# The splits of a first expert's weight pieces moved later, and a mask copy moved ahead of a copy of results, in a fused retention, mixture and attention kernel

## The chip, the core and the metric

The kernel runs on one core of a Trainium2 chip. The core has five engines that run side by side, each with its own in-order stream of instructions: TensorE (PE in the profile, with its weight loads as PEld), VectorE (DVE), ScalarE (ACT), GpSimd (POOL) and SyncE (SP, which here only issues DMA transfers). They meet through semaphores. The metric is the device time of one execution, in microseconds (us).

## The reference

Three layers follow one another, all in float32: a retention layer (a running state per head), a layer of eight experts in which each token goes to one expert, and an attention layer with four gated heads.

```python
def _attn_ref(q, k, v):                       # B, H, S, D = 2, 8, 768, 64
    for t in range(S):
        state = gamma * state + outer(k[:, :, t], v[:, :, t])
        y[:, :, t] = scale * (q[:, :, t] @ state)

def _moe_ref(x, w_gate, w_local, w1, w2):     # 8 experts, 512 -> 1024 -> 512
            fresh_e = int(np.argmax(logits[b, s]))
            e = fresh_e if s == 0 or local_gate[b, s] < 0.5 else prev_e
            prev_e = e
            h = np.maximum(x[b, s] @ w1[e], 0.0)
            out[b, s] = p[e] * (h @ w2[e])

def _moe2_ref(x, w_gate, wq, wk, wv, wo):     # 4 attention heads, each token weighs the top 2
```

The expert of a token can hang on the token before it (it keeps the last expert unless its local gate says otherwise), so the routing is a scan along the sequence.

## The kernel before

**Retention and routing.** The sequence is cut into six chunks of 128 positions, two batches each. A loop runs over the first five chunks; the sixth is written out by hand behind it. In chunk c the engines compute the outputs of chunk c (`outputs_past`, `outputs_now`), copy them out of PSUM (`evacuate`, on ACT), update the state (`state`, `keep`), and work on the routing of chunk c - 1 in a class `Route`: `first` (DVE) finds the mask of tokens that keep their expert and the fresh choices; `keeps` and `fresh` (PE) turn both masks; `spread` (ACT) copies the turned mask out of PSUM into `rs`; `held` and `count` (DVE) are scans along the tokens; `offset` (PE) adds the counts of earlier chunks; `rank`, `slots`, `hots` and `table` build the table of which token sits at which place of which expert. The table, the offsets and the places stand in one PSUM tile, pB, of which `pTab` is a part.

In the last chunk V is the routing of the fifth chunk, W that of the fourth and U that of the sixth. Once V's and W's part of the table is there, the rows of the first expert are gathered (`gather(0, GE)`, POOL), while U is still worked out; U's tokens are added to the gathered block by matmuls (`late`). The block is copied out as a high half x0h (ACT) and the remainder x0l (DVE).

**Weights in two halves.** Each expert's weights come in eight pieces of 128x1024 (pieces 0 to 3 of the first matrix, 4 to 7 of the second). `fetch_piece(i)` (SP) loads the raw piece into one of five buffers, `split_high(i)` (ACT) rounds it to `whi`, and `split_low(i)` (DVE) writes the remainder `wlo`. Three products stand for one: whi with the high half of x, wlo with it, and whi with the low half. Since raw buffers turn over five by five, piece 5 is loaded into the buffer that piece 0 leaves, 6 into that of 1, 7 into that of 2, 8 into that of 3, and a fetch waits until its forerunner's `split_low` has read it.

**Order.** The loop, the last chunk and the experts are recorded under a manual schedule: each engine runs its instructions in the order in which the code issues them. PSUM tiles of kind "B" rotate through three buffers: pS, pR and pB hold them in the first layer, then `warm`, then the four results `ph` of the first expert's first matrix, so that the second `ph` (piece 1) takes the buffer of pB and the fourth that of the first.

The first expert multiplies at L900 (first matrix, 24 matmuls a piece) and L948 (second matrix). Behind U's part of the table stand, on DVE, the ordering of the experts (`PM` to `OD`), a `split_low(2)`, the copy `tf` of the finished table out of pB (L781), the gather lists and `split_low(3)`.

Of the kernel before, what the change touches and what calls it, by code (L numbers as in the profile page):

```python
# [24 lines left out]
NC = S // C  # L25
# [87 lines left out]
def kernel(  # L113
# [57 lines left out]
    def fetch_piece(i):  # L171
        if i >= NP:
            return
        e, r = divmod(i, 8)
        raws[i] = ring.tile([128, 1040], F32, name="wraw", bufs=RAWS)[:, :1024]
        src = w1 if r < 4 else w2
        if e:
            if e > len(ords):
                n = slice(1, 2) if e == 1 else slice(2, E)
                ords.extend(nc.values_load_multi_w_load_instructions(  # L180
                    OD[0:1, n], engines=[mybir.EngineType.SP], min_val=0, max_val=E - 1)[1])
            src = src[bass.ds(ords[e - 1], 1), r % 4].rearrange("e p n -> (e p) n")
        else:
            src = src[e, r % 4]
        nc.sync.dma_start(raws[i], src)

    def split_high(i):
        hi = ring.tile([128, 1024], F32R, name="whi", bufs=PIECES)
        lo = ring.tile([128, 1024], F32R, name="wlo", bufs=PIECES)
        nc.scalar.activation(hi, raws[i], AF.Copy)  # L190
        pieces[i] = (hi, lo)

    def split_low(i):
        hi, lo = pieces[i]
        nc.vector.tensor_tensor(out=lo, in0=raws.pop(i), in1=hi.bitcast(F32), op=OP.subtract)  # L195
# [48 lines left out]
    with tc.tile_pool(name="s1", bufs=2) as s1:  # L244
# [9 lines left out]
        def load_pair(c, x):  # L254
            if c >= NC:
                return
            for b in range(B):
                load_half(c * B + b, x)
# [55 lines left out]
        def fade(n, j):  # L314
            nc.vector.tensor_tensor(out=AM[n][:, j], in0=PA[n][j], in1=DT[:, j], op=OP.mult)
# [26 lines left out]
        def outputs_past(c):  # L342
            pY = [bank("C", [128, 2 * B, C]) for _ in range(2)]
            if c:
                for b in range(B):
                    for g in range(2):
                        for r, j in ((0, 0), (1, 1), (0, 1), (1, 0)):
                            k = 2 * g + j
                            nc.tensor.matmul(pY[r][half(j), 2 * b + g, :], SB[b][half(r), k, :],
                                             QD[B * c + b][half(r), k * C:(k + 1) * C], start=b == 0 and g == 0, stop=False,  # L350
                                             skip_group_check=True)
            return pY

        def outputs_now(c, pY, r):
            for b in range(B):
                x = XB[B * c + b, 1]
                for g in range(2):
                    for j in range(2):
                        h = 4 * g + 2 * r + j
                        nc.tensor.matmul(pY[r][half(j), 2 * b + g, :], x[:, 1, h * D:(h + 1) * D],  # L360
                                         AM[B * c + b][:, r, 2 * g + j, :], start=c == 0, stop=True, skip_group_check=True)

        def evacuate(c, pY, r):
            XT[c, r] = s1.tile([128, 2 * B, C], F32, name="xT")
            nc.scalar.activation(XT[c, r], pY[r], AF.Copy)
# [4 lines left out]
        def state(n):  # L370
            c, b = divmod(n, B)
            if c == NC - 1:
                return
            for k in range(H // 2):
                for r in range(2):
                    h = k // 2 * 4 + r * 2 + k % 2
                    nc.tensor.matmul(pS[half(r), b, k, :], KD[n][:, h, :], XB[n, 1][:, 1, h * D:(h + 1) * D],
                                     start=c == 0 and b == 0 and k == 0, stop=True, skip_group_check=True)

        def keep(n):  # L380
            c, b = divmod(n, B)
            if c == NC - 1:
                return
            nc.scalar.activation(SB[b], pS[:, b], AF.Copy)
# [24 lines left out]
        def put_rows(pv):  # L409
            for dst, src in zip(rows_of(XRT[:, :, E:]), pv):  # L410
                nc.scalar.activation(dst, src, AF.Copy)

        def send_rows(n):
            c, b = divmod(n, B)
            t = b * S + c * C + 1
            nc.sync.dma_start(x1_d[t:t + C, :], XRT[:, b])
# [124 lines left out]
        with tc.manual_schedule(engines={ENG.PE, ENG.DVE, ENG.Activation, ENG.Pool, ENG.SP}):  # L541
# [11 lines left out]
            def turn(c):  # L553
                part, logits, pv = turn_pair(c)
                l2 = s1.tile([128, B, E + 1], F32, name="l2")
                part(0, 8)
                return lambda: [logits(b, l2) for b in range(B)], pv

            for c in range(NC - 1):
                load_pair(c + 2, 0)  # L560
                if c >= NC - 3:
                    fetch_piece(3 * (c - NC + 3))
                if c == NC - 2:
                    split_high(0)
                if c:
                    sums, pv = turn(c - 1)
                if c >= 2:
                    RT[c - 2].columns()
                    RT[c - 2].slots(0, B)
                    RT[c - 2].marks(0, B)  # L570
                    RT[c - 2].tokens(0, B)
                if c >= 3:
                    RT[c - 3].table(0, B)
                if c:
                    sums()
                    put_rows(pv)
                    for b in range(B):
                        send_rows(B * (c - 1) + b)
                    RT[c - 1] = Route(c - 1)
                    RT[c - 1].first(LL[c - 1], 0, B)  # L580
                if c >= 2:
                    RT[c - 2].hots(0, B)
                if c == NC - 2:
                    split_low(0)
                if c == 2:
                    nc.sync.dma_start(x1_d[0:1, :], ZR[0:1])
                    for b in range(B):
                        t = b * S + (NC - 1) * C + 1
                        nc.sync.dma_start(x1_d[t:t + C, :], ZR)
                ns = [B * c + b for b in range(B)]  # L590
                nn = [n + B for n in ns]
                pY = outputs_past(c)
                for r in range(2):
                    outputs_now(c, pY, r)
                    evacuate(c, pY, r)
                for n in ns:
                    state(n)
                if c:
                    RT[c - 1].keeps()
                    RT[c - 1].fresh()  # L600
                    RT[c - 1].spread()
                    RT[c - 1].held()
                    RT[c - 1].count()
                for n in ns:
                    keep(n)
                if c == NC - 2:
                    split_high(1)
                    split_high(2)
                for f in (decay_q, decay_k):
                    for n in nn:  # L610
                        f(n)
                load_pair(c + 2, 1)
                if c == 1:
                    nc.gpsimd.memset(ZR, 0.0)
                if c >= NC - 3:
                    for i in ((1, 2), (4,))[c - NC + 3]:
                        fetch_piece(i)
                next_qt(c + 2)
                scores(nn[0], "A")
                for r in range(2):  # L620
                    fade(nn[0], r)
                scores(nn[1], "C")
                if c:
                    RT[c - 1].offset()
                    RT[c - 1].rank()
                for r in range(2):
                    fade(nn[1], r)
                if c:
                    RT[c - 1].shares(LL[c - 1], 0, B)
            c = NC - 1  # L630
# [14 lines left out]
                fetch_piece(i)  # L645
            V = RT[c - 1] = Route(c - 1)
            V.first(LL[c - 1], 0, B)
            split_low(1)
            pY = outputs_past(c)
            U = Route(c)  # L650
            xs = [s1.tile([128, B, DM], F32R, name="blq", bufs=4) for _ in range(2)]
# [36 lines left out]
                                     start=False, stop=m == 1 and b == 1, skip_group_check=True)  # L688

            outputs_now(c, pY, 0)  # L690
            evacuate(c, pY, 0)
            V.keeps()
            V.fresh()
            V.spread()
            V.held()
            V.count()
            W.hots(0, B)
# [67 lines left out]
            for x in range(2):  # L765
                n = slice(2 * x, 2 * x + 2)
                nc.vector.tensor_tensor(out=X0[1][:, n, :], in0=acc[x], in1=X0[0][:, n, :].bitcast(F32),
                                        op=OP.subtract)
            nc.vector.tensor_tensor(out=PM, in0=rk[:, None, :].to_broadcast(sq),
                                    in1=cn("place")[:, :, None].to_broadcast(sq), op=OP.is_equal)  # L770
            one = s1.tile([1, 2, E, E], F32, name="one")
# [752 lines left out]
```

## Time and profile before

| | us |
|---|---|
| three runs | 388.18, 388.53, 390.83 (median 388.53) |
| the profiled execution, whole | 387.61 |
| its span in the trace | 385.8 |
| PE busy | 371.9 (96% of the span) |
| DVE busy | 282.8 (73%) |
| ACT busy | 233.4 (60%) |
| POOL busy | 123.3 (32%) |

All times of a trace are counted from the start of the span; an execution is 1.81 us longer than its span here (387.61 - 385.8). A busy share is a mean over layers with different limits. The retention layer ends at about 67 us of the span, the experts at about 250 us, and attention takes the rest. Rows of a timeline merge neighbours of one kind; the duration of a merged row reaches from the first start to the last end.

### The profile page before, as it was taken

What the parts mean: (1) busy time and instruction counts of PE and PEld (TensorE: products, weight loads), DVE (VectorE), ACT (ScalarE), POOL (GpSimd) and SP (SyncE); (2) the same over time, 40 slices, a digit from 0 to 9 for tenths busy, and PEclk for the clock granted to TensorE, in tenths of its full rate; (3) what the DMA queues carried; (4) which work ended last, traced back from release to release, by engine and by line L of the source; (5) the groups of instructions that cost most, each with busy time, mean ns of one, the idle gap of its engine ahead of it and who ended that gap; (6) DMA issues with size and microseconds to landing.
All of it is one profiled execution on the core that took longest, in us unless ns stands there. A gap on an engine that the chain in (4) does not pass through costs nothing.

```text
span 385.8 us, 8560 instructions
## 1 busy us (share of the span) xinstructions
PE 371.9 (96%) x3020; PEld 326.0 (84%) x3020; DVE 282.8 (73%) x783; ACT 233.4 (60%) x547; POOL 123.3 (32%) x172
## 2 busy tenths in 40 slices
PE   7999888999999999999999999999999999999993
PEld 3999777989989797889898898989889988988782
DVE  5589887885767868788888991578976876678741
ACT  1555563464647656587777781557866765759641
POOL 2775312151514022131310022434445422515420
PEclk9999999999999999999999999999999999999998
DMA  7999964696785667778776752131120001000111
GB/s 251 400 405 338 398 235 148 172 299 238 229 304 179 226 239 242 243 235 274 244 245 232 246 220 96 51 110 58 29 72 21 21 0 57 0 30 27 56 58 62
DMA packets 23610, 67.39 MB, mean 175 GB/s; under 512 B 4469, under 2 KB 4725, under 8 KB 23560
## 3 DMA queue, kind: packets, MB, share of 16 engines
q1 hardware_dynamic: 21010, 59.34, 44.9%
q0 software_dynamic: 2544, 7.42, 5.6%
q8 instruction: 26, 0.43, 0.4%
q14 instruction: 24, 0.20, 0.2%
q10 hardware_dynamic: 6, 0.01, 0.0%
HBM read 56.16 MB, written 11.07 MB: 174 GB/s over the span
## 4 chain that ended last, share of the span: by engine, by line
PE 88%; DMA 6%; issue 2%; DVE 1%; ACT 1%; SPq 0%; POOL 0%; POOLq 0%; ACTq 0%; DVEq 0%
PE C L948 19%; PE B L900 9%; PE C L1100 8%; PE B L912 5%; PE C L1285 5%; PE B L1265 5%; PE A L1209 4%; PE C L1138 4%; PE C L1306 4%; PE A L912 3%; PE C L360 3%; PE B L914 2%; PE C L944 2%; DMA x_d<-y,SI 2%; DMA blk<-in_blk_dram 2%
## 5 line engine op out<-in xcount | busy, mean ns | idle before, releaser
L195 DVE TENSOR_TENSOR wlo<-wraw,whi 128x1024 fp32r<-128x1024 f32 x64 | 77.0, 1223 | 15.7 <-ACT whi L190 15.6
L190 ACT ACTIVATE whi<-wraw 128x1024 fp32r<-128x1024 f32 x64 | 65.6, 1050 | 3.0 <-DMA wraw<-in_w_dram 2.9
L970 POOL DMA_INDIRECT x_d<-y,SI x16 | 19.9, 1243 | 125.1 <-ACT y L960 80.5
L1243 POOL TENSOR_SCALAR a<-a,mx,wt 128x128 f32<-128x128 f32 (+5 forms) x48 | 33.9, 716 | 51.5 <-PE B L1265 12.0
L1232 ACT ACTIVATE a<-a,mx 128x128 f32<-128x128 f32 (+5 forms) x48 | 32.2, 670 | 23.0 <-DVE mx L1222 19.6
L948 PE MATMUL C<-whi,hh 128*128 128x512 f32 (+4 forms) x112 | 45.5, 407 | 0.0
L948 PE MATMUL C<-whi,hl 128*128 128x512 f32 (+4 forms) x112 | 44.2, 394 | 0.0
L948 PE MATMUL C<-wlo,hh 128*128 128x512 f32 (+4 forms) x112 | 44.2, 394 | 0.0
L912 PE MATMUL B<-xx,whi 128*128 128x384 f32 (+3 forms) x100 | 31.0, 365 | 0.0
L1265 PE MATMUL B<-K,a 128*128 128x128 f32 x168 | 26.4, 274 | 0.0
L1222 DVE CUSTOM_DVE_ANT_0 a<-A,MR 128x384 f32<-128x384 f32 (+3 forms) x48 | 25.3, 530 | 1.5 <-PE A L1209 0.9
L914 PE MATMUL B<-xx,wlo 128*128 128x192 f32 (+3 forms) x100 | 25.5, 255 | 0.0
L948 PEld LDWEIGHTS C<-whi,hl 128*128 128x128 f32 (+4 forms) x112 | 20.0, 179 | 6.0
L948 PEld LDWEIGHTS C<-wlo,hh 128*128 128x128 f32 (+4 forms) x112 | 20.1, 180 | 5.0
L948 PEld LDWEIGHTS C<-whi,hh 128*128 128x128 f32 (+4 forms) x112 | 20.1, 179 | 4.7
L886 ACT ACTIVATE hh<-t 128x128 fp32r<-128x128 f32 (+4 forms) x56 | 16.3, 318 | 12.1 <-DVE t L918 11.8
L1265 PEld LDWEIGHTS B<-K,a 128*128 128x128 f32 x168 | 19.9, 140 | 2.6 <-issue 0.7
L224 POOL DMA_INDIRECT xg<-x_d,GI x14 | 16.4, 1173 | 17.5 <-DVE hl L902 13.5
L1209 PE MATMUL A<-ks,qh 128*128 128x256 f32 (+3 forms) x56 | 21.5, 384 | 0.0
L1285 PE MATMUL C<-at,vv 128*64 128x256 f32 (+1 forms) x204 | 20.6, 347 | 0.0
L912 PEld LDWEIGHTS B<-xx,whi 128*128 128x128 f32 x100 | 18.8, 188 | 0.7
L914 PEld LDWEIGHTS B<-xx,wlo 128*128 128x128 f32 x100 | 19.1, 191 | 0.2
(327 smaller groups left out, 963.1 us busy)
## 6 DMA issues: line engine op xcount, KB each, us to landing
wraw<-in_w_dram SPq DMA_DIRECT2D x64, 512.0 KB, 4.8
blq<-in_blk_dram SPq DMA_DIRECT2D x12, 512.0 KB, 8.6
blk<-in_blk_dram SPq DMA_DIRECT2D x12, 512.0 KB, 8.2
x_d<-xr SPq DMA_DIRECT2D x12, 260.0 KB, 6.0
out_dram<-y SPq DMA_DIRECT2D x12, 256.0 KB, 2.0
xr<-x_d SPq DMA_DIRECT2D x10, 256.0 KB, 2.6
x_d<-ZR SPq DMA_DIRECT2D x2, 260.0 KB, 5.4
wraw<-in_wv_dram SPq DMA_DIRECT2D x1, 520.0 KB, 5.8
```

The costliest lines, as they stand in the source:

```text
L190: nc.scalar.activation(hi, raws[i], AF.Copy)
L195: nc.vector.tensor_tensor(out=lo, in0=raws.pop(i), in1=hi.bitcast(F32), op=OP.subtract)
L900: nc.tensor.matmul(ph[:, a, :N], w[:, k, n], x[:, k, :N], start=m == 0, stop=m == 11)
L912: nc.tensor.matmul(pa[:, :, :N], wh[:, k, n], XX[e][:, k, :, :N], start=k == 0, stop=False, skip_group_check=True)
L914: nc.tensor.matmul(pa[:, 1, :N], wl[:, k, n], XX[e][:, k, 0, :N], start=False, stop=k == 3, skip_group_check=True)
L948: nc.tensor.matmul(pys[i][:rows], h[:, a, n], w[:, a, :], start=f == 0 and a == 0 and m == 0, stop=f == 3 and a == 1 and m == 2)
L1100: nc.tensor.matmul(pp, w[:, k, a * 128:(a + 1) * 128], x[:, k, :], start=m == 0, stop=m == 11)
L1209: nc.tensor.matmul(ps[:, :w], qq[b, g, e][:, tq], KS[b, e][:, s0:s0 + w], start=m == 0, stop=m == 1)
L1232: nc.scalar.activation(AA[u][:, :n], AA[u][:, :n], AF.Exp, bias=mx[:, 0, i:i + 1], scale=-1.0, accum_out=mx[:, 1, i:i + 1])
L1243: nc.gpsimd.tensor_scalar(a[:, :n], a[:, :n], mx[:, 1, i:i + 1], WT[b, g][:, i, e:e + 1], op0=OP.mult, op1=OP.mult)
L1265: nc.tensor.transpose(pT[:, s - s0, :], a[:, s * C:(s + 1) * C], ident)
L1285: nc.tensor.matmul(po[j * HD:(j + 1) * HD, r], VV[b, s][:, e * HD:(e + 1) * HD], at[j][:, s, r], start=s == 0, stop=s == ns - 1, skip_grou ...
```

## The change

The three high halves of pieces 0 to 2 are now all made behind the state copies of the fifth chunk (c == 4, `NC - 2`); before, the first stood at the start of that chunk. `split_low(0)` moves from the fifth chunk to the place in the last chunk where `split_low(1)` stood, and `split_low(1)` moves behind the two x0l subtractions, ahead of `PM`. In the last chunk, `V.spread()` now stands ahead of `evacuate(c, pY, 0)` on ACT.

```diff
@@ fifth chunk (c == NC - 2) @@
-                if c == NC - 2:
-                    split_high(0)
                 if c:
                     sums, pv = turn(c - 1)
...
                     RT[c - 2].hots(0, B)
-                if c == NC - 2:
-                    split_low(0)
...
                 for n in ns:
                     keep(n)
                 if c == NC - 2:
-                    split_high(1)
-                    split_high(2)
+                    for i in range(3):
+                        split_high(i)
@@ last chunk @@
             V.first(LL[c - 1], 0, B)
-            split_low(1)
+            split_low(0)
...
             outputs_now(c, pY, 0)
-            evacuate(c, pY, 0)
             V.keeps()
             V.fresh()
             V.spread()
+            evacuate(c, pY, 0)
             V.held()
...
                 nc.vector.tensor_tensor(out=X0[1][:, n, :], in0=acc[x], in1=X0[0][:, n, :].bitcast(F32),
                                         op=OP.subtract)
+            split_low(1)
             nc.vector.tensor_tensor(out=PM, in0=rk[:, None, :].to_broadcast(sq),
```

ACT, from the state copies of the fifth chunk (SB) to the exponentials of the last (PP); whi is a high half, xr the copy of the rows, rs the copy of the turned mask, xT the copies of results:

```order
 L384 ACTIVATE SB_119<-B 128x256
-L190 ACTIVATE whi<-wraw 128x1024 x2
+L190 ACTIVATE whi<-wraw 128x1024 x3
 L453 ACTIVATE PP,DN<-L,nm 128x8 x2
 L411 ACTIVATE xr<-C 128x384
 L411 ACTIVATE xr<-A 128x2x128
 L411 ACTIVATE xr<-A 128x384
-L365 ACTIVATE xT<-C 128x512
 L480 ACTIVATE rs<-B 128x128
-L365 ACTIVATE xT<-C 128x512
+L365 ACTIVATE xT<-C 128x512 x2
 L453 ACTIVATE PP,DN<-L,nm 128x8 x2
```

The third high half has come behind the state copies, and rs has passed the first of the two copies of results.

DVE, at the end of the last chunk, before the change; x0l is the low half of the gathered block, wlo a weight's low half (piece 2's here), tf the copy of the table out of pB:

```order
118 L767 TENSOR_TENSOR x0l<-C,x0h 128x512 x2
119 L769 TENSOR_TENSOR PM<-rk,K 128x64
120 L772 TENSOR_TENSOR one<-PM,K 1x64
121 L775 TENSOR_REDUCE pick<-one 1x8
122 L776 CAST OD<-pick 1x8
123 L195 TENSOR_TENSOR wlo<-wraw,whi 128x1024
124 L781 COPY tf<-B 128x16
```

The same place with the change:

```order
117 L763 TENSOR_TENSOR x0l<-C,x0h 128x512 x2
118 L195 TENSOR_TENSOR wlo<-wraw,whi 128x1024
119 L766 TENSOR_TENSOR PM<-rk,K 128x64
120 L769 TENSOR_TENSOR one<-PM,K 1x64
121 L772 TENSOR_REDUCE pick<-one 1x8
122 L773 CAST OD<-pick 1x8
123 L195 TENSOR_TENSOR wlo<-wraw,whi 128x1024
124 L778 COPY tf<-B 128x16
```

Piece 1's low half now stands between x0l and PM, so tf has two low halves ahead of it instead of one.

## Rows read from the trace of the kernel before

**Rows 1.** The page, part 4: the chain that ended last, by engine

```profile
PE 88%; DMA 6%; issue 2%; DVE 1%; ACT 1%; SPq 0%; POOL 0%; POOLq 0%; ACTq 0%; DVEq 0%
```

**Rows 2.** That chain from 53 to 92 us: start us, us, what

```profile
60.21 3.40 DMA xg<-x_d,GE
...
68.06 11.56 PE B L900 x94
...
85.21 0.44 PE A L835 x4
```

**Rows 3.** PE timeline, last chunk: start us, us, work [idle before, releaser]

```profile
54.86 0.22 PE L476 MATMUL B<-IB,fo 128*128 128x128 bf16 x1
...
57.14 0.16 PE L495 MATMUL B<-rc,OM 128*128 128x1 bf16 x1 [1.04 <-DVE oh L525]
```

**Rows 4.** ACT timeline, last chunk

```profile
54.97 0.60 ACT L365 ACTIVATE xT<-C 128x512 f32<-128x512 f32 x1 [0.76 <-PE C L360]
55.46 0.27 ACT L480 ACTIVATE rs<-B 128x128 f32<-128x128 f32 x1
```

**Rows 5.** DVE timeline, last chunk

```profile
54.23 1.22 DVE L195 TENSOR_TENSOR wlo<-wraw,whi 128x1024 fp32r<-128x1024 f32 x1
55.77 0.48 DVE L485 TENSOR_TENSOR_SCAN rc<-rs,rc,B 128x128 bf16<-128x128 f32 x1 [0.32 <-ACT rs L480]
```

**Rows 6.** Timelines of DVE and PE, fifth chunk

```profile
47.68 1.21 DVE L195 TENSOR_TENSOR wlo<-wraw,whi 128x1024 fp32r<-128x1024 f32 x1
...
49.32 0.42 DVE L489 TENSOR_TENSOR_SCAN rc<-B,rc 128x128 bf16<-128x128 f32 x1
...
50.29 0.18 PE L495 MATMUL B<-rc,OM 128*128 128x2 bf16 x1
```

**Rows 7.** ACT timeline, fifth chunk and start of the last

```profile
44.22 0.49 ACT L411 ACTIVATE xr<-C 128x384 f32<-128x384 f32 x1 [0.25 <-DVE l L398]
...
48.78 2.02 ACT L190 ACTIVATE whi<-wraw 128x1024 fp32r<-128x1024 f32 x2
...
52.49 0.30 ACT L453 ACTIVATE PP<-L,nm 128x8 f32<-128x8 f32 x1 [1.70 <-DVE nm L451]
```

**Rows 8.** DVE timeline, end of the last chunk and first expert

```profile
68.65 0.22 DVE L769 TENSOR_TENSOR PM<-rk,K 128x64 f32<-128x64 f32 x1
...
69.46 1.21 DVE L195 TENSOR_TENSOR wlo<-wraw,whi 128x1024 fp32r<-128x1024 f32 x1
70.60 0.15 DVE L781 COPY tf<-B 128x16 f32<-128x16 f32 x1
...
74.95 0.69 DVE L902 SCALAR_TENSOR_TENSOR hl<-B,hh 128x512 fp32r<-128x512 f32 x1 [0.88 <-DMA x_d<-PP]
```

**Rows 9.** PEld timeline, the first expert's first matrix

```profile
70.18 0.54 PEld L900 LDWEIGHTS B<-x0l,whi 128*128 128x128 f32 x4
70.81 0.53 PEld L900 LDWEIGHTS B<-x0h,whi 128*128 128x128 f32 x4
71.27 0.55 PEld L900 LDWEIGHTS B<-x0h,wlo 128*128 128x128 f32 x4
...
76.49 0.55 PEld L900 LDWEIGHTS B<-x0h,whi 128*128 128x128 f32 x4
```

**Rows 10.** SP queue timeline; landing of line L416 there; the page, part 6

```profile
65.79 0.82 SPq L416 DMA_DIRECT2D x_d<-xr  x2
70.70 0.34 SPq L185 DMA_DIRECT2D wraw<-in_w_dram  x1
...
DMA to landing us min/median/max: 2.1/2.3/2.7
...
x_d<-xr SPq DMA_DIRECT2D x12, 260.0 KB, 6.0
```

**Rows 11.** POOL timeline: the gather for the second expert

```profile
76.05 1.96 POOL L224 DMA_INDIRECT xg<-x_d,GI  x1 [13.53 <-DVE hl L902]
```

**Rows 12.** Stretch 56 to 57.2: us, PE, PEld, DVE, ACT, POOL busy, PEclk, DMA, GB/s

```profile
56.00:57.20 1.20, 0.16 (x5) 0.15 (x3) 1.13 (x5) 0.60 (x2) 0.00 (x0) 1.00 0.79 258
```

## The prediction

> **What bounds the kernel now.** I read the chain that ended last first: PE carries 88% of it [rows 1], so what the change is worth is what it does to PE's start in the stage that it touches, and whether PE waits behind that. The piece of the chain for that stage shows two things. From the last chunk's routing to the first expert the chain runs through small steps, and a gather of 3.40 us stands in it [rows 2]; a step ahead of the gather that ends earlier brings all of it forward. From 68.06 us on PE runs through L900, L948 and the turning of the next expert's rows at 85.21 [rows 2], so a delay of PE behind 68 us is not made up for there, and one ahead of it is carried on as well. The timelines of the single engines then tell what each step waits for.
>
> Two waits of PE matter. At 57.14 the offset matmul starts after 1.04 us without work, and its releaser is the last DVE step of a row that starts from the copied mask rs [rows 3]: rs, the two scans, the mask table `oh`. And at 70.81 the first weight load of piece 1 is late: groups of four loads follow each other at 0.46 (70.81 to 71.27), so it was due at about 70.64, behind 70.18; it came 0.06 after the table copy tf ended (70.60 + 0.15 = 70.75) [rows 8, 9]. The result `ph` of piece 1 takes the PSUM buffer of pB, which tf reads last. So PE already waits, for some 0.15 us, on the place in DVE's stream into which the change puts another low half.
>
> **The fifth chunk: nothing.** The first high half leaves ACT's stream ahead of xr, but xr waited for DVE's logits anyway, with 0.25 us of idle time in front of it [rows 7]; nothing is gained. Made as a third copy behind the state copies, at the spacing of the two there ((2.02 - 1.05) = about 0.97 us each), it ends near 51.8, and ACT next has work at 52.49, after 1.70 us without any [rows 7]. The cover is that wait for DVE; without it the price would be 0.97 us on ACT. On DVE a low half of 1.21 us goes, which stood between the mask table and the scans [rows 6]. The second scan ended at 49.74 (49.32 + 0.42), and PE asked for it at 50.29, in its own order, with no wait [rows 6]. So an earlier scan brings PE nothing: 0, where the bound would be one low half, 1.14 us, had PE been waiting there.
>
> **rs ahead of the copy of results: a gain of 0.34 us.** rs started at 55.46, 0.49 behind xT, though the masks on PE ended at 55.08 (54.86 + 0.22) [rows 3, 4]. Put first, it can start at about 55.12 (a releaser's step costs 0.04 here) and end at 55.39, not 55.73. The scan `held` behind it started at 55.77 after 0.32 us of waiting for rs [rows 4, 5]. It can now start at 55.43; DVE's low half (now piece 0's, of the same size) lets the next step in by 54.23 + 1.14 = 55.37 [rows 5], so the low half nearly binds but does not. Gain: 55.77 - 55.43 = 0.34 us. The bounds are 0 (if the low half ends later than that) and 0.40. The gain reaches PE, since the offset waits for this row, and PE has been without other work since 56.10 (57.14 - 1.04) [rows 3]; then all up to the gather and its 3.40 us follows PE. The copy of results that rs passes ends by 55.99 (55.39 + 0.60), and its first reader, the gate's matmuls, stands behind the offset at 56.80, so it hides there.
>
> **Piece 1's low half ahead of PM: a loss of 1.14 us.** It stands in front of four small steps, then piece 2's low half, then tf. One low half holds DVE for 1.14 us from its start to the next step's (69.46 to 70.60) [rows 8]. All of it is DVE time with no idle stretch to take it up, and tf moves by it in full, against the x0l ahead of it. Counted with the gain, x0l ends 0.34 earlier, the low half runs from 68.31 (68.65 - 0.34) to 69.45, and tf ends at 70.75 - 0.34 + 1.14 = 71.55. PE has finished piece 0 at 70.64 - 0.34 = 70.30, and waits for 1.3 us instead of 0.15; its load starts at 71.61, not 70.81.
>
> The spacing comes from the row. The Trainium skill (VectorE: DVE Perf Modes, section "The DRAIN you can't avoid") says that the next operation doesn't start until the pipe has emptied, which would make the price the full duration, 1.21 us, and the net loss 0.87; the trace shows the next step starting 0.07 us ahead of that end, so its 1.14 stands.
>
> Does PE make that up later? Its next gates move by the same amount. The fourth result's load at 76.49 needs the first `hl`, which ended at 75.64 (74.95 + 0.69), 0.85 us earlier [rows 8, 9]; both move by 0.80. The low halves of the second matrix and the gathers for the second expert keep their distance too. So the loss is carried: net 1.14 - 0.34 = **+0.80 us**.
>
> **What is queued behind the waits.** The buffer of piece 0 is read later now, but fetch 5 still goes out near 55.5. Fetch 6 needs piece 1's buffer, and so waits until 69.5. SP is in order: the sends of the last rows (at 65.79 before) come out near 69.9 and 70.3, fetch 7 (at 70.70, behind piece 2's low half) near 71.5, and the shares behind it near 72 [rows 10]. Who waits for the sends: the first expert's hh and hl, whose memory they still read, and the gather for the second expert. A send took at most 2.7 us to land in this stretch, and 6.0 in the median of all twelve [rows 10]. With 2.7 the second lands at 73.0, well ahead of hl at 75.75 (74.95 + 0.80). With 6.0 it lands at 76.3, hl ends 0.55 to 0.6 later, and the 0.85 us of room ahead of the fourth result still covers it. I take the lower end, as that row is of the same sends, and count 0. The gather for the second expert started at 76.05 and its rows are needed at 85.21 [rows 2, 11], 9.2 us later, where the first gather took 3.40; the need moves by 0.80, so 2 us of delay fit as well.
>
> **The sum.** Against the profiled execution: 387.61 - 0.34 + 1.14 = 388.41. That execution lies 0.92 us under the median of the runs, so I add the same difference to the median: 388.53 + 0.80 = **389.3 us**, 0.2% slower. A measurement of this kernel can tell a change of about 1% (3.9 us) from none; three runs alone spread over 2.65 us.
>
> **Rivals.** *The table copy doesn't hold PE.* If the late load at 70.81 was due to something else than tf, and piece 1's result needs nothing from DVE's tail, only the gain is left: 388.53 - 0.34 = 388.2, not slower than before. For it: the profile names no wait of PE there. Against it: the load comes 0.06 behind tf, about the step of any release in these rows, and the buffers' rotation says the same. Decided by whether tf's end is followed by that load. Chance 0.14.
>
> *The blocked SP queue decides.* Fetch 6 and the sends go out together, 1 MB at once, and the sends land later than even the twelve's median, at 77.5 to 78. Then hl waits for them, the fourth result's load comes some 1 to 1.5 us later still, and the time is 390.3 to 390.8. It decides from a landing time of about 6.2 us on. Against it: the 2.7 us in the same stretch. Chance 0.14.
>
> *PE's longer wait costs it its clock.* If the 1.3 us without matmuls took the granted clock from 2.4 to 1.2 GHz, the next piece (six groups of 0.47, 2.8 us) would take twice as long, and with a second piece at the low level the loss is 5.6: 392.1 to 394.9, slower. Against it: from 56.0 to 57.2 PE was busy for 0.16 us only, and the clock stood at 1.00, the level of 2.4 GHz [rows 12]. The Trainium skill (TensorE: Matmul & The Clock Gate, Part 1) has the clock fall after the engine has been idle; these rows show no fall after a wait of nearly the same length. Chance 0.04.
>
> **How the numbers follow.** The forecast, a net loss between 0.3 and 1.3 us, has 0.66; the rest, 0.02, is for a gain that I don't see. The range reaches from the first rival less the scatter of a median (0.3) to the second rival's upper end: 387.9 to 390.9. Faster by over 1% needs 3.9 us, which no step has to give: 0.02. Slower by over 1% needs the clock, or the queue at far more than its price: 0.04. Within 1%: 0.94.
>
> **What would show it.** In the profile of the changed kernel: rs ahead of xT and starting within 0.1 us of the masks; held 0.3 earlier and the gather near 59.9; a PE gap of about 1.3 us ahead of piece 1's first load, ending with tf; the sends on SP near 70 and no new wait in front of hl. I am wrong if that gap is missing, if the gather starts at 60.2 as before, or if the gap is there but the expert that follows ends no later.

## The result and the profile after

| | us |
|---|---|
| kernel before, 18 runs | 389.03 median (387.62 to 390.83) |
| changed kernel, 18 runs | 390.7 median (389.36 to 394.89) |
| ratio | 1.0053, 95% interval 1.0036 to 1.0069 |
| profiled execution of the changed kernel, whole / span | 390.85 / 389.1 |

The change costs 0.53%, about 2.06 us of 389.03 (1.40 to 2.68 by the interval). The sign is the forecast's and the changed kernel's median lies in its range, but the loss is some two and a half times the 0.80 us of its sum.

**Start-up first.** The span grew by 3.3 us (389.1 - 385.8), but not all of that is the change's. The offset matmul of the fifth chunk, ahead of all that changes in the last chunk, already starts at 51.67 and not at 50.29 [rows 6]. The same point shifts by -1.08 to +3.43 us over the profiles of this study, with moved splits and without. So all times below are compared with this start-up shift (1.38 us here) taken off. That point stands behind the edit in the fifth chunk, so the edit there needs an earlier one: PE's last wait ahead of the first moved high half (42.91 before), first in the kernel before, then in the changed kernel.

```profile
41.83 0.63 PE L395 MATMUL C<-IW,xT 128*128 128x137 f32 x4 [1.44 <-issue]
...
43.22 0.63 PE L395 MATMUL C<-IW,xT 128*128 128x137 f32 x4 [1.29 <-issue]
```

From there to the fifth chunk's offset it is 8.46 us before (50.29 - 41.83) and 8.45 with the change (51.67 - 43.22): nothing gained and nothing lost there in these two profiles.

PE's timeline of the changed kernel (start us, us, work, [idle before, releaser]), from the fifth chunk to the second expert:

```profile
51.67 0.18 PE L495 MATMUL B<-rc,OM 128*128 128x2 bf16 x1
...
56.25 0.22 PE L476 MATMUL B<-IB,fo 128*128 128x128 bf16 x1
...
58.19 0.16 PE L495 MATMUL B<-rc,OM 128*128 128x1 bf16 x1 [0.70 <-DVE oh L525]
...
72.92 0.75 PE L897 MATMUL B<-x0h,whi 128*128 128x256 f32 x4 [1.01 <-DVE tf L778]
...
88.24 0.66 PE L832 MATMUL A<-K,xg 128*128 128x128 f32 x4 [0.92 <-DMA xg<-x_d,GI]
```

The offset stands at 58.19 - 1.38 = 56.81, against 57.14 [rows 3]: the gain of 0.33. The last two lines are two waits that before did not have by name: 1.01 us for tf ahead of piece 1, which was forecast, and 0.92 us for the rows of the second expert, which was not.

ACT's timeline of the changed kernel, at the masks:

```profile
56.51 0.28 ACT L480 ACTIVATE rs<-B 128x128 f32<-128x128 f32 x1 [0.90 <-PE B L476]
56.68 0.59 ACT L365 ACTIVATE xT<-C 128x512 f32<-128x512 f32 x1
```

rs follows the masks (56.25 + 0.22 = 56.47) by 0.04, ahead of xT; in [rows 4] it stood behind.

DVE's timeline of the changed kernel, at the end of the last chunk:

```profile
69.63 1.21 DVE L195 TENSOR_TENSOR wlo<-wraw,whi 128x1024 fp32r<-128x1024 f32 x1
70.76 0.22 DVE L766 TENSOR_TENSOR PM<-rk,K 128x64 f32<-128x64 f32 x1
...
71.58 1.20 DVE L195 TENSOR_TENSOR wlo<-wraw,whi 128x1024 fp32r<-128x1024 f32 x1
72.71 0.15 DVE L778 COPY tf<-B 128x16 f32<-128x16 f32 x1
...
77.07 0.69 DVE L899 SCALAR_TENSOR_TENSOR hl<-B,hh 128x512 fp32r<-128x512 f32 x1 [0.88 <-DMA wraw<-in_w_dram]
```

The added low half sets PM back by 1.13 (69.63 to 70.76). tf ends at 72.86, and PE starts piece 1 at 72.92. hl, the low half of the first result, starts at 77.07 - 1.38 = 75.69, against 74.95 [rows 8]: 0.74 later, no more than PE itself.

SP's queue in the changed kernel (a merged row reaches from the first issue to the last):

```profile
56.87 14.33 SPq L185 DMA_DIRECT2D wraw<-in_w_dram  x2
71.38 0.82 SPq L416 DMA_DIRECT2D x_d<-xr  x2
72.81 0.34 SPq L185 DMA_DIRECT2D wraw<-in_w_dram  x1
75.64 1.08 SPq L426 DMA_DIRECT2D x_d<-PP  x2
...
79.89 3.18 SPq L185 DMA_DIRECT2D wraw<-in_w_dram  x4
```

Two SP waits of the changed kernel, in 71 to 73 and in 75 to 79 us (line and releaser: us in total, times, longest):

```profile
SPq L185 <- DVE PM L766: 13.7, 1, 13.7
...
SPq L426 <- DMA x_d<-xr: 2.6, 2, 2.4
```

The first row of the queue is fetches 5 and 6 (pieces 5 and 6): the second of them waits 13.7 us for piece 1's low half. The wait is put down to PM, the next step on DVE, but fetch 6 goes out at 70.87, right behind the low half's end (69.63 + 1.21 = 70.84) and ahead of PM's (70.76 + 0.22 = 70.98). The sends (L416) behind it start at 70.00 with the shift off, 4.2 us later than at 65.79 [rows 10]. The shares (L426) then wait 2.4 us more, for the sends to land.

What comes of that is in the chain that ended last of the changed kernel, 70 to 110 us (start us, us, what):

```profile
69.71 1.13 DVE wlo L195
70.84 0.15 DVE PM L766
70.99 0.21 SPq L185
...
71.38 0.34 SPq L416
...
71.82 4.47 DMA x_d<-xr
...
76.34 3.17 DMA x_d<-PP
...
80.31 0.35 POOL xg L224
...
86.74 7.57 issue
...
94.55 7.10 DMA x_d<-y,SI
...
104.30 4.79 DMA xg<-x_d,GI
...
109.13 0.66 PE A L832 x4
```

Piece 1's low half, fetch 6, the sends, the shares, the gather for the second expert: the chain runs through SP here, where before it ran through PE [rows 2]. In this execution it then stays on POOL, over 7.57 us for which it names no releaser, and reaches PE only at the third expert's rows, so it shows the order of these steps and not what they cost PE at the second expert. The second profile of this kernel, below, has the chain go from that gather straight to PE. The share of PE in the whole chain says little: it is 88% before [rows 1] and 80% here, but in a second profile of the kernel before, without an edit, it is 71% (part 4 of the pages, by engine: changed kernel, then the kernel before again):

```profile
PE 80%; DVE 6%; DMA 5%; issue 4%; ACT 1%; POOL 1%; SPq 0%; POOLq 0%; DVEq 0%; ACTq 0%
...
PE 71%; ACT 9%; DVE 8%; DMA 6%; issue 4%; POOL 0%; POOLq 0%; ACTq 0%; SPq 0%; DVEq 0%
```

POOL's timeline of the changed kernel at that gather:

```profile
80.31 1.53 POOL L224 DMA_INDIRECT xg<-x_d,GI  x1 [16.70 <-DVE hl L899]
```

The releaser named, hl, had ended 2.55 us ahead (77.07 + 0.69 = 77.76). The chain tells the true one, the shares' landing (76.34 + 3.17 = 79.51). The time from this issue to landing, in the changed kernel:

```profile
DMA to landing us min/median/max: 7.9/7.9/7.9
```

And of the same gather in the kernel before:

```profile
DMA to landing us min/median/max: 5.9/5.9/5.9
```

Before, the rows landed at 76.05 + 5.9 = 81.95, and PE asked for them at 85.05 (the first of the group in [rows 2], on PE's timeline): 3.1 us of room. After, the gather starts 2.88 later (80.31 - 1.38 - 76.05) and takes 2.0 longer, while PE comes only 0.73 later. 2.88 + 2.0 - 3.1 - 0.73 = 1.05 us too late, and PE, 0.73 late at the second matrix, is 1.80 late there.

### The profile page after: what moved, and what is told of

Same layout as the page of the kernel before. It is cut to its first block, busy times and chain, and to the rows that moved or that the text cites. A ratio compares the mean times of both kernels' runs of the same rounds, so it can differ in the third digit from the quotient of the medians.

```text
span 389.1 us, 8559 instructions
## 1 busy us (share of the span) xinstructions
PE 374.4 (96%) x3020; PEld 326.8 (84%) x3020; DVE 283.1 (73%) x783; ACT 233.3 (60%) x547; POOL 123.5 (32%) x172
## 4 chain that ended last, share of the span: by engine, by line
PE 80%; DVE 6%; DMA 5%; issue 4%; ACT 1%; POOL 1%; SPq 0%; POOLq 0%; DVEq 0%; ACTq 0%
PE C L945 17%; PE C L1097 8%; PE B L909 5%; PE B L1262 5%; PE C L1282 5%; PE A L1206 4%; PE C L1135 4%; PE C L1303 4%; PE A L909 3%; PE B L897 3%; PE B L911 2%; PE A L311 2%; PE C L941 2%; PE C L360 2%; DMA x_d<-y,SI 2%
```

## The experiments

The theory: two terms add up, tf behind one more low half (net +0.8 at piece 1), and the sends held behind fetch 6 on SP, which make the gather for the second expert late. The rivals: the sum at tf is all and the rest is scatter, or bytes (fetches 6 and 7 beside sends and gather), not order, slow the gather.

Single executions of this kernel spread over several us, so a ratio of 12 runs carries an interval of about ±0.25% (1 us). Each ratio below is against runs of the kernel before that were taken beside it, with its 95% interval in brackets. The terms are read from the profiles: the same PE instructions, start in the kernel named less start in the first profile of before, less the start-up shift (first column). The points by their times before: offset 57.14, piece 1 70.81, second matrix 79.46, rows of the second expert 85.05, rows of the third 105.04, a point past the experts 252, the end of the span. The last column is the start of the gather for the second expert, shift off (76.05 before).

| us | start-up | offset | piece 1 | 2nd matrix | 2nd expert | 3rd expert | 252 | end | gather |
|---|---|---|---|---|---|---|---|---|---|
| before again | 0.37 | 0.00 | 0.02 | 0.03 | 0.04 | 0.05 | -0.04 | 0.18 | 76.03 |
| changed | 1.38 | -0.33 | 0.73 | 0.73 | 1.80 | 2.70 | 2.07 | 1.92 | 78.93 |
| changed again | 1.24 | -0.33 | 0.81 | 0.80 | 1.27 | 1.32 | 0.65 | 0.98 | 79.17 |
| rs first alone | 0.35 | -0.34 | -0.20 | -0.19 | -0.18 | 0.42 | 0.24 | 0.22 | 75.94 |
| splits moved alone | 0.17 | 0.00 | 1.29 | 1.28 | 2.57 | 3.65 | 3.03 | 3.05 | 79.89 |
| changed, tf first | -1.08 | -0.34 | -0.32 | 0.49 | 0.91 | 1.85 | 1.85 | 2.07 | 79.79 |
| changed, 6 and 7 behind shares | 1.20 | -0.34 | 0.92 | 0.92 | 0.92 | 1.62 | 1.01 | 0.88 | 72.80 |
| changed, 6 behind sends | 3.43 | -0.34 | 0.92 | 0.91 | 0.91 | 1.60 | 1.16 | 0.89 | 77.95 |
| changed, early gather | 2.60 | -0.34 | 0.81 | 0.81 | 1.54 | 1.59 | 1.62 | 1.61 | 79.23 |
| rs first, tf first | 3.24 | -0.28 | -0.29 | -0.39 | -0.39 | -0.38 | -0.59 | -0.55 | 75.94 |
| all three | 2.94 | -0.34 | -0.34 | -0.44 | -0.43 | -0.42 | -0.91 | -0.90 | 75.95 |
| all three again | 1.84 | -0.34 | -0.45 | -0.55 | -0.54 | -0.53 | -0.72 | -0.72 | 75.71 |

**The kernel before, again** (no edit).

> The kernel before, unchanged, for a second profile. Question: is PE's wait at the turning of the third expert's rows, 0.9 us with the change and none in the profile of before, the change's doing? Theory now (it is not, or only in part: with rs first alone it was 0.6 us, and POOL's step from the second scatter to that gather varies): this profile shows a wait of 0.4 to 0.8 us there too. Rival (the change makes all of it): no wait there, and the turn at the distance from the start of the second expert that the first profile shows, within 0.2 us.

One run, 388.16. Shift off, PE's points agree with the first profile to 0.05 us up to 105 us: that is how finely the table can be read there, and the wait at the third expert's rows that was expected (0.4 to 0.8 us) is not there. Behind it the points wander more: this profile is 0.63 late near the experts' end (235.5) and has that back at 252. That point is the first turning of attention's rows, for which the first profile waits:

```profile
251.75 0.63 PE L1083 MATMUL C<-K,xr 128*128 128x128 f32 x4 [0.49 <-DMA xr<-x_d]
```

A profile without this wait has up to 0.65 us back there, so in such profiles the last two columns hold less than was lost in the experts.

**rs first alone.**

```diff
             outputs_now(c, pY, 0)
-            evacuate(c, pY, 0)
             V.keeps()
             V.fresh()
             V.spread()
+            evacuate(c, pY, 0)
```

> The kernel before with one edit, rs ahead of the first copy of results on ACT; all splits stand where they stood. Theory (the change's loss comes wholly from the late low half of piece 1, and rs first is a gain): PE's offset matmul and the gather behind it come 0.3 to 0.4 us earlier against the steps ahead of them, and nothing takes it back: ratio to before 0.9990, within 0.9980 to 1.0000. Rival (the earlier routing collides with the sends and gives the gain back): ratio 1.000 or above, with the gather's DMA longer than 3.4 us by what was gained.

Ratio 0.9987 (0.9955 to 1.002). The offset gains 0.34, as forecast; 0.20 of it is left where PE starts on x0h (68.06 before) and at piece 1, so 0.14 is given back between the offset and the first expert; where, is open. The whole time shows no difference that can be told from none.

**The splits moved alone.**

```diff
+            evacuate(c, pY, 0)
             V.keeps()
             V.fresh()
             V.spread()
-            evacuate(c, pY, 0)
```

(against the changed kernel)

> The changed kernel with the copy of results ahead of rs again, so the moved splits alone. Theory: the changed kernel's loss and, on top, the 0.34 to 0.42 us that rs first had gained: 2.4 us over before, ratio 1.0063 (1.0045 to 1.0080); PE still waits about 1.0 us for the table copy and about 0.9 us for the gather of the second expert. Rival (rs first is part of the loss): ratio at or under the changed kernel's 1.0053 by more than 0.001.

Ratio 1.0035 (1.0012 to 1.0059). That is below the 1.0045 to 1.0080 of the theory and, by its median, on the side of the rival; but the interval overlaps the changed kernel's (1.0036 to 1.0069), so the times decide nothing between them. The profile speaks for the theory: at every point from piece 1 to the end it is later than either profile of the changed kernel. The offset is where it was (0.00): without rs first there is no gain in the last chunk. Piece 1 loses 1.29, of which 0.16 stood at x0h already: 1.13, the price of one low half. Then 1.29 more is lost at the second expert, where the gather starts 3.84 later than before. By the profile, the whole loss comes with this part of the change.

**The table copy first**, with the change.

```diff
+            tf = s1.tile([128, 2, E], F32, name="tf", bufs=1)
+            nc.vector.tensor_copy(tf, pTab)
             split_low(1)
...
-            tf = s1.tile([128, 2, E], F32, name="tf", bufs=1)
-            nc.vector.tensor_copy(tf, pTab)
```

> The changed kernel with the table copy tf ahead of piece 1's low half, right behind x0l; the SP queue is as in the changed kernel. Theory (two gates in a row, and the gather for the second expert, held back by the blocked SP queue, is the later one): PE's wait of 1.0 us ahead of piece 1 goes to nothing, its wait at the turning of the second expert's rows grows from 0.9 to 1.9 us or more, and the time stays within 0.3 us of the changed kernel's: ratio to before 1.0045 to 1.0060. Rival (the two losses add up, each its own): the time falls by 1.1 us, ratio 1.0025.

Ratio 1.0037 (1.0014 to 1.006). The wait at piece 1 is gone (-0.32), which shows that tf was its cause. But at the second matrix PE is 0.49 late all the same. The weight loads of this kernel:

```profile
73.00 0.54 PEld L897 LDWEIGHTS B<-x0h,whi 128*128 128x128 f32 x4 [0.79 <-DVE one L790]
```

Its DVE timeline at that step:

```profile
71.61 1.22 DVE L195 TENSOR_TENSOR wlo<-wraw,whi 128x1024 fp32r<-128x1024 f32 x1
72.75 0.20 DVE L790 TENSOR_TENSOR one<-PM,B 1x64 f32<-1x64 f32 x1
```

The third result needs the buffer of `warm`, which `one` reads last, behind the next low half (72.75 + 0.20 = 72.95, load at 73.00). So the low half holds DVE's whole tail: with tf out of its way the price is paid one buffer later, 0.81 there. The wait at the second expert stays, as SP was not touched, but it is smaller (0.42), where the theory had it grow to 1.9. The gather starts 0.9 later than in the changed kernel (79.79 against 78.93), but PE begins on its rows 6.2 us behind that start, not 7.9; why they land sooner is open. The rival's 1.0025 lies in the interval too, so the time does not decide between them.

**Fetches 6 and 7 behind the shares**, with the change.

```diff
-            for i in (5, 6):
-                fetch_piece(i)
+            fetch_piece(5)
...
-            fetch_piece(7)
...
+            for i in (6, 7):
+                fetch_piece(i)
```

(the last place is behind the stores of the shares and of the zero rows)

> The changed kernel with the fetches of pieces 6 and 7 moved behind the sends of the last rows, the shares and the cleared rows on SP; all else as in the changed kernel. Theory (the blocked SP queue costs 1.1 us at the first gather and up to 0.9 at the second): the sends go out near 67 to 68 instead of 71.4, the gather for the second expert starts 5 to 6 us earlier, when its list is ready, PE waits for no gather, and only the wait for the table copy (1.0 us) is left: 0.5 to 0.9 us over before, ratio 1.0013 to 1.0025. Rival (the gather is late because its list is made later on DVE, not because of SP): the gather starts within 1 us of where it did and the ratio stays at 1.005.

Ratio 1.004 (1.0014 to 1.0065), against 1.0013 to 1.0025 expected. The gather starts at 72.80, 6.1 earlier than in the changed kernel, and nothing is lost at the second expert (0.92 before it and at it), while the loss at tf stands; at the third expert PE still loses 0.70, where no wait for a gather was expected. That the late gather comes from SP's order is shown. The whole time does not show it: by its interval this kernel is no faster than the changed one, though its profile ends 1.04 ahead of the changed kernel's first and 0.10 ahead of its second.

**Fetch 6 behind the sends only**, with the change.

```diff
-            for i in (5, 6):
-                fetch_piece(i)
+            fetch_piece(5)
...
-            fetch_piece(7)
+            for i in (6, 7):
+                fetch_piece(i)
```

> The changed kernel with the fetch of piece 6 alone moved, from ahead of the sends of the last rows to behind them (it still goes out at the same time, since it waits for piece 1's low half; fetch 7 and the shares stay behind it). Theory (the shares waited for the landing of sends that the blocked fetch had held back): sends some 4 to 5 us earlier against the steps around them, no wait of the shares for them, the gather for the second expert starts near 77 on the time of the first profile, 2 us earlier than with the change, and PE waits for it no longer; the wait for the table copy stays. 0.7 to 1.1 us over before at the second expert's start. Rival (it is the bytes of fetch 6 that are in the way, issued at 71): the gather starts as late as with the change, or lands as late, and PE's wait of 0.9 us stays.

Ratio 1.0007 (0.9986 to 1.0029), with its upper end under the lower end of the changed kernel's. That much is more than the profile has: its points agree with those of the kernel with fetches 6 and 7 behind the shares, timed at 1.004, to 0.15 us. SP's queue in this kernel:

```profile
69.05 0.81 SPq L416 DMA_DIRECT2D x_d<-xr  x2
73.09 2.29 SPq L185 DMA_DIRECT2D wraw<-in_w_dram  x2
75.55 0.99 SPq L426 DMA_DIRECT2D x_d<-PP  x2
```

POOL's timeline in it, at the gather:

```profile
81.37 1.00 POOL L224 DMA_INDIRECT xg<-x_d,GI  x1 [15.71 <-DMA x_d<-PP]
```

Issue to landing, for the second of the two gathers there:

```profile
DMA to landing us min/median/max: 5.5/5.5/5.5
```

With its shift of 3.43 off, the sends go out at 65.62, the gather at 77.95, 1.9 later than before (1.0 ahead of the changed kernel's, where 2 was expected), and it is in time: nothing is lost at the second expert (0.91 and 0.91). Fetches 6 and 7 still go out between sends and shares, so their bytes alone don't make it late: what differs is whether the sends wait behind fetch 6. A start 1.9 later fits into the room of 3.1 us, with a landing of 5.5; one 2.9 later, with a landing of 7.9, does not. Why the landing differs was not tried by itself.

**The changed kernel again** (no edit).

> The changed kernel, for a second profile. Theory: the same three places as in the first: rs first 0.33 us earlier at the offset, 1.1 us lost at the second piece, 1.0 to 1.2 us lost at the turning of the second expert's rows. Open: the wait at the third expert's rows (0.9 us in the first profile, 0.7 to 1.0 in all three kernels with the splits moved so far) and how much of it is given back at the end of the experts. Rival (one of the waits was chance of that execution): one of them differs by more than 0.4 us.

One run, 389.76. POOL's timeline of this second execution of the changed kernel:

```profile
80.41 1.37 POOL L224 DMA_INDIRECT xg<-x_d,GI  x1 [16.94 <-DVE hl L899]
```

Its waits of PE, 60 to 250 us:

```profile
PE B L897 <- DVE tf L778: 1.0, 1, 1.0
PE A L832 <- DMA xg<-x_d,GI: 0.3, 1, 0.3
```

The chain that ended last in it:

```profile
71.75 4.50 DMA x_d<-xr
...
76.30 3.31 DMA x_d<-PP
...
80.41 7.10 DMA xg<-x_d,GI
...
87.55 0.66 PE A L832 x4
```

Here the chain goes from the sends over the shares and the gather into PE, which starts 0.04 behind the landing (80.41 + 7.10 = 87.51). Both waits are there again, tf's to 0.1 the same and the gather's smaller (0.47 against 1.07 in the table). The wait for the third expert is not. The terms of the loss are not one number but 0.8 and 0.5 to 1.1.

**The early gather**, with the change. The table has a second new wait in the first profile of the changed kernel, 0.90 at the third expert's rows. Its gather stands on POOL behind the first expert's two scatters (changed kernel, first profile):

```profile
94.55 1.28 POOL L967 DMA_INDIRECT x_d<-y,SI  x1 [7.81 <-ACT y L957]
102.46 1.53 POOL L967 DMA_INDIRECT x_d<-y,SI  x1 [6.63 <-DMA x_d<-y,SI]
104.30 1.05 POOL L224 DMA_INDIRECT xg<-x_d,GI  x1 [0.30 <-issue]
```

The second scatter waits for the first to land, and the gather waits behind both. So the experiment issues the gather between them, in the first expert's output step.

```diff
-            if e < 2:
+            if e < 1:
                 gather(e + 1, None)
                 gather(e + 1, GI)
...
+                if i and not e:
+                    gather(2, None)
+                    gather(2, GI)
```

> The changed kernel with one edit: the gather for the third expert stands on POOL ahead of the first expert's second scatter, not behind it. Theory (that gather is late because POOL first waits for the landing of the first scatter, some 7 us): it starts near 95 instead of 104, PE's wait of 0.9 us for it goes, and 0.3 to 0.9 us remain to the end: ratio to before 1.0030 to 1.0045. Rival (the gather is slow by itself, or the scatters behind it are then late): the wait stays, or the end of the experts comes no earlier.

Ratio 1.005 (1.0023 to 1.0077). The gather goes out at 94.47 with the shift off, and the wait at the third expert is gone (1.54 before it, 1.59 at it). The whole time is none the better for it. By 252 us both profiles of the changed kernel have 0.63 and 0.67 back, the one without that wait too (2.70 to 2.07, 1.32 to 0.65), and this one has nothing back (1.59 to 1.62), as it waits for attention's rows at that point (0.34, where neither profile of the changed kernel does): what the early gather gains is no more than executions differ by at that wait.

**rs and tf first, splits as before.** The edit of rs first alone, and the tf copy of the table copy first, both on the kernel before.

> The kernel before with two edits: rs ahead of the first copy of results, and tf ahead of PM; all splits as before. Theory: rs first gives 0.34 us, tf first takes away the 0.15 us that PE waited for tf, and the gates behind keep room: 0.5 us less than before at the start of the first expert's second matrix, of which the wait at the third expert's rows takes back what it binds; ratio 0.9985 (0.9970 to 1.0000). Rival (the next gate, the third result's buffer, takes the gain of tf first): the gain at the second matrix is 0.34 us or less.

Ratio 0.9988 (0.9962 to 1.0013). From x0h (-0.25 there) to the second matrix (-0.39) this kernel gains a further 0.14, which agrees with the 0.15 us by which the load of piece 1 was late before [rows 9]. The gain is carried to the third expert without loss.

**All three**: the edit above and the early gather, on the kernel before.

> The kernel before with rs first, tf first and the early gather for the third expert. Theory: the 0.5 us of the first two is kept past the third expert's rows, and the usual wait there (0.4 to 0.6 us) goes as well: ratio 0.9975 (0.9955 to 0.9995). Rival (the end of the experts hangs on the scatters, which come later now): no faster than with the first two alone.

Ratio 0.9976 (0.9955 to 0.9997).

> The kernel with rs first, tf first and the early gather for the third expert, timed again. Theory: ratio 0.9975 again, within 0.9955 to 0.9995, and 0.4 us gained at the start of the second expert. Rival (the first measurement was scatter): ratio 0.999 or above.

Ratio 1.0003 (0.9976 to 1.0031) for the same kernel. Both profiles carry a gain of 0.42 to 0.54 to the third expert; the whole time is not shown to be faster, as one interval ends just below 1 and the other contains it.

## Why the prediction was right and wrong

**rs ahead of the copy of results: right, and to its size.** -0.33 or -0.34 at the offset in nine of the ten profiles that have it (-0.28 in the tenth), 0.00 in both that don't. **The fifth chunk: right as far as is seen**: 8.46 us before and 8.45 with the change from the point ahead of it. In both profiles of the kernel before it is 8.46; with other waits in that chunk the same distance is 8.95 in the second profile of the changed kernel and 9.02 with the splits alone, but also 8.20 to 9.14 in kernels whose splits were not moved.

**Piece 1's low half: right.** 1.14 forecast; from x0h to piece 1, 1.13 (from -0.40 to 0.73) and 1.14 (from -0.33 to 0.81) in the two profiles of the changed kernel, 1.13 with the splits alone. The load of piece 1 was forecast for 71.61 and came at 72.92 - 1.38 = 71.54. The rival "the table copy doesn't hold PE" is refuted by the table copy first. That DVE's next step comes 1.13 after the start of a low half, not 1.21, holds in the rows after as well.

**The clock: right.** The window 72 to 74 us of the changed kernel (us, busy of PE, PEld, DVE, ACT, POOL, PEclk, DMA share, GB/s):

```profile
72.00:74.00 2.00, 1.08 (x9) 1.08 (x10) 1.86 (x9) 0.00 (x0) 0.00 (x0) 1.00 0.97 271
```

Nearly half of it without matmuls, and the granted clock at 1.00, the level of 2.4 GHz.

**"What is queued behind the waits": wrong.** This step counted 0, and it is the one that failed. It had the sends at 69.9 and 70.3 (measured 70.0 and 70.4), but put the shares "near 72". It took them as queued behind fetch 7 alone. They also wait for the sends to land, and go out at 75.64 - 1.38 = 74.26. It took 2.7 us for a landing and got 4.47, between its two ends. And it took the room of the gather for the second expert from the first gather's 3.40: 9.2 - 3.40 = 5.8 us, of which it called 2 safe. That gather's own landing was 5.9 us already before, which leaves 3.1; the delay was 2.88 and the landing 7.9. So its sentence that the gathers "keep their distance too" fails as well. The term measured 1.07 and 0.47 in the two profiles of the changed kernel, 1.29 with the splits alone, 0.42 and 0.73 with the table copy first and with the early gather, and 0 in both kernels whose SP order let the sends go first.

**The rival "the blocked SP queue decides"** had the mechanism up to the late sends, but the wrong victim, hl, and a chance of 0.14. That its size fits (390.3 to 390.8, with 390.7 measured), and that the range reached so far, is in part luck: it priced a wait of 1 to 1.5 us at hl, and the wait was another one, of 0.47 to 1.07. Neither hl nor hh, the high half of the same result that ACT makes ahead of it, was held, though the profile puts hh's wait down to the sends (ACT's timeline, the kernel before, then the changed kernel):

```profile
74.33 0.60 ACT L901 ACTIVATE hh<-B 128x512 fp32r<-128x512 f32 x1 [5.37 <-DVE OV L800]
...
76.44 0.60 ACT L898 ACTIVATE hh<-B 128x512 fp32r<-128x512 f32 x1 [6.50 <-DMA x_d<-xr]
```

hh starts 3.52 us behind piece 1 here (76.44 - 72.92) and 3.52 behind it before (74.33 - 70.81), so it moved with PE, and hl with it. It was near: the sends landed at 76.29 (71.82 + 4.47), 0.15 ahead of hh.

**The first premise, PE's share of the chain, is weaker than it looked.** The 88% [rows 1] is of one execution; the same kernel has 71% in its second profile. PE's own points, up to the third expert, agree in the two to 0.05 us, and the sum rests on those.

**What stays open.** The terms shown at the second expert sum to 1.27 and 1.80 in the changed kernel's two profiles, and their ends lie 0.98 and 1.92 late; the timed loss is 1.40 to 2.68. The wait at the third expert, which the prediction does not have at all, adds 0.90 in one of the two. It is there in five of the seven profiles with moved splits (the early gather takes it out of a sixth), and in one of the four others without the early gather, so whether the change causes it or only makes it likelier isn't settled. That execution-to-execution part may also be why the kernel with fetches 6 and 7 behind the shares, which loses nothing at the second expert, is not measurably faster than the changed one; it isn't shown. No kernel was run with both the table copy first and the sends ahead of fetch 6, so that the two terms are the whole loss is not shown by taking both away.

## What to carry to other kernels

When a step that frees a buffer is moved later, follow the load that waits for that buffer: on a DMA queue that issues in order, as SP's does here, it holds every transfer behind it, and the victim can be several steps on (here low half, fetch, sends, shares, gather). Price the room of such a victim with the landing time of its own row in its own stretch, not with a quiet one's, and list what each queued transfer itself waits for. Where one of several waits on the same busy engine is removed, look at the next step in that engine's order before counting it as won.

## What the runs showed of the hardware

The same indirect gather took 5.9 us to land in the kernel before, 7.9 and 7.1 in the two profiles of the changed kernel, where weight fetches went out 0.42 and 0.45 us ahead of it (79.89 to 80.31, 79.96 to 80.41), and the gather ahead of the first expert took 3.40 [rows 2]; that the fetches are the reason was not tried by itself. The two sends of 260 KB took 2.3 us in the median before [rows 10], and the second of them 4.47 when it went out right behind fetch 6. Two executions of the same kernel differ by up to 1.1 us in their start-up here (1.84 and 2.94 for all three), over all profiles by 4.5 us, so a profile's whole span tells nothing of a change of this size.
